# Ten normalising steps on a third engine, and a new written-out order: a one-core transformer block on Trainium2

## The chip, the core and the metric

The kernel runs on one core of a Trainium2 chip. A core has engines that work side by side and wait for one another through semaphores: TensorE (PE, matrix products, with weight loads PEld), VectorE (DVE), ScalarE (ACT), GpSimd (POOL) and SyncE (SP), which issues the transfers. The metric is the device time of one execution in microseconds (us). Every engine executes its own instructions in the order in which the program lists them.

## The reference

One block over x, 2048 positions by 512 channels, in bfloat16, with shift, scale and gate rows computed from a condition vector `c`:

```python
h = _layernorm(x) * (1 + ca) + sa
x = x + ga * _A_ref(h, A_wqkv, A_wo)     # attention over 8 keys: positions s, s-2, ..., s-14
h = _layernorm(x) * (1 + cb) + sb
x = x + gb * _B_ref(h, ...)              # layernorm again, then an MLP over the POSITIONS:
                                         # u = gelu(h^T w1 + b1), y = u w2 + b2
```

The attention has 32 heads of 16 channels. The MLP mixes the 2048 positions through 1792 hidden units, so that it needs all positions of the normalised h.

## The kernel before

The positions come in 16 tiles of 128 rows and in 4 chunks of 4 tiles. Every tile passes three normalisations, so there are 48 normalising steps, each of one 128x512 tile:

- `ln1n0` to `ln1n15`: the first layernorm, from `xx` into `n_sb`. PE then transposes a chunk (`tr`), and the eviction `hT` applies scale and shift.
- `t0` to `t15`: the second layernorm, from the updated `xx` into `h2`. `aff` on DVE then applies scale and shift to the whole chunk in two products.
- `h3_0` to `h3_15`: the MLP's own layernorm, from `h2` into `h3`, which the MLP's matmuls read.

A normalising step needs mean and reciprocal deviation, from `ln1s` and `ln3s` (statistics), `rstd` (ACT) and `nb` (DVE).

For each chunk, PE makes q, k and v (`qkvq`, `qkvk`, `qkvv`), evicted by `evq`, `evk`, `evv`. DVE multiplies q with the 8 shifted keys in four large key products (`qk0_0` to `qk0_3` in chunk 0, one 128x4096 product each). PE sums them within heads (`red`), DVE takes the maximum (`max`), PE subtracts it (`sub`), ACT takes the exponential (`exp`), PE sums (`sum`), `rb` and `smul` divide, `a2_` spreads the weights over partitions, `a2ev` evicts them. Copies of v shifted by position are made by 16 transfers a chunk (`vd`); DVE multiplies them with the weights (`pv`, four a chunk), PE sums (`pvacc`), `oev` evicts, and `wo` projects. `x1ev` adds the result to x. When `x1ev` stands on ACT, the addition of the old x is one more matmul with the identity in `wo`; on DVE it is part of the step.

The MLP's first layer (`mlp1_0_..` over the first 8 tiles, `mlp1_1_..` over the others) runs in between as soon as `h3` tiles are there: `mlp1_0_10_0` reads tiles 0 to 3. `park` keeps its first half; `gadd`, `gelu`, `gbm` finish it, `mlp2` is the second layer, `fin` and `st_out` write the result. PSUM is four slots of two banks (`ps`), which all these steps share.

The order is written out by hand in the string `ORDER`: one word for each step, with the engine after a colon where a step can run on more than one (`v` DVE, `a` ACT, `g` POOL), and the PSUM slot for the steps that open one. `schedule` (line 147) walks it, and the steps are issued in that order, so that it sets the order on each engine and in SP's queue of transfers.

Of the kernel before, what the change touches and what calls it, by code (L numbers as in the profile page):

```python
# [8 lines left out]
ALU = mybir.AluOpType  # L9
# [5 lines left out]
S, D, H, DH, NW, DIL, F = 2048, 512, 32, 16, 8, 2, 1792  # L15
# [14 lines left out]
ln1n0:v modcols_h ln1n1:a nb1_0_2 ln1n3:v modcols1 ln1n2:v ld_wo1 tr0_00:2 tr0_02 ld_wmod5 modcols_cp tr0_10:3 hT0_0:v  # L30
tr0_12 ln1s7:a warm1:1 hT0_2:v hT0_1:v ld_x3 hT0_3:v qkvk0_0:0 ln1s6:a ln1s5:v qkvk0_0b qkvk0_2:2 ld_wmod2 ln1s4:v
evk0_0:a sc_rep rstd1_1_0 ln1s10:v ld_wo2 qkvk0_1:1 evk0_2:a ld_wo3 nb1_1_0 ln1s11:v qkvq0_0:3 ln1n5:a ln1n7:v
qkvq0_2:0 ln1s8:v evk0_1:a ln1n4:a khalo1 ln1s9:v ld_b1 evq0_0:a ln1n6:v rstd1_2_0 ld_wmod4 qk0_0 tr1_10:2 evq0_2:a
ld_wmod3 tr1_00:1 qkvq0_1:3 hT1_2:a ld_wo0 hT1_0:a qkvv0_0:0 nb1_2_0 qk0_2 hT1_3:a evq0_1:a hT1_1:a qkvv0_2:2 evv0_0:a
qk0_1 ln1n10:a qkvq1_0:3 evv0_2:a ln1n8:v ln1s15:a vd0_020 qk0_3 qkvk1_0:1 vd0_001 vd0_011 evq1_0:a red0_0:0 vd0_021
evk1_0:a ln1s12:v red0_1 vd0_000 red0_2 ln1s14:a ln1n11:v vhalo1 red0_3 qk1_0 vd0_131 qkvk1_2:2 vd0_010 ln1n9:a
vd0_121 ln1s13:a vd0_030 qkvq1_2:3 max0 ld_b2 evk1_2:a qk1_1 sub0 evq1_2:a qkvv1_0:1 khalo2 vd0_031 exp0 vd0_101 qk1_2
rstd1_3_0 vd0_111 sum0 tr2_00:2 vd0_130 rb0 red1_0:3 hT2_0:a vd0_120 red1_1 nb1_3_0 smul0 vd0_110 evv1_0:a red1_2
qk1_3 a2_0:0 vd0_100 hT2_1:a tr2_10:1 a2ev0:a qkvv1_2:2 hT2_2:a pv0_0 ln1n14:a red1_3 hT2_3:a modrows:0 ln1n13:a
qkvq2_0:1 pv0_1 mrow_ev evv1_2:a bc0 ln1n12:a biascols:0 vd1_130 pvacc0_0:2 biascols_cp ln1n15:a max1 pvacc0_1 vd1_021  # L40
evq2_0:a vd1_100 tr3_00:0 pv0_3 vd1_010 sub1 oev0_1:a qkvv2_0:1 vd1_011 exp1 vd1_020 vd1_030 pv0_2 hT3_0:a sum1
vd1_000 qkvk2_0:2 evv2_0:a vd1_001 hT3_1:a vd1_031 gmul rb1 vd1_110 pvacc0_2:1 evk2_0:a pvacc0_3 vd1_120 tr3_10:0
smul1 vd1_101 oev0_3:a qk2_1 a2_1:3 vd1_131 hT3_2:a wo2:2 vd1_111 a2ev1:a vd1_121 wo3:1 x1ev2:a bc1 qk2_0 bc2 hT3_3:a
wo0:3 x1ev3:a vhalo2 x1sq2 wo1:2 bc3 pv1_0 x1sq3 qkvq3_0:0 x1ev1:a x1ev0:a x1sq1 pv1_1 pvacc1_0:1 x1sq0 qkvk2_2:2
rstd2_0_0 evq3_0:a nb2_0_0 pv1_2 pvacc1_1 evk2_2:a qkvv2_2:3 t0:a khalo3 ld_w1_0_1 t1:a t2:v pv1_3 qkvq2_2:0 t3:a
oev1_1:a pvacc1_2:2 evv2_2:a aff0_0 pvacc1_3 qkvk3_0:1 evq2_2:a vd2_120 vd2_030 oev1_3:a vhalo3 qk2_2 vd2_020
ln3s0_3:a wo5:3 vd2_010 wo4:0 vd2_021 x1ev5:a vd2_011 evk3_0:a qk2_3 wo7:2 ld_w1_0_3 x1ev4:a vd2_000 wo6:3 x1sq5
vd2_131 x1ev7:a vd2_121 ln3s0_0:v red2_0:1 x1sq4 red2_1 vd2_031 ln3s0_2:v red2_2 vd2_111 x1sq7 red2_3 ln3s0_1:v
# [5 lines left out]
red3_3 mlp1_0_11_4 mlp1_0_10_4 max3 vd3_120 mlp1_0_31_4 park0_1:a mlp1_0_01_4 pv2_1 sub3 pvacc2_0:1 exp3 mlp1_0_00_4
pv2_2 vd3_101 sum3 vd3_100 pvacc2_1 rb3 vd3_121 mlp1_0_30_4 oev2_1:a vd3_130 smul3 mlp1_0_60_0:3 park0_3:a vd3_110
pv2_3 a2_3:1 ld_w1_0_4 pvacc2_2:2 vd3_111 a2ev3:a mlp1_0_61_0 vd3_131 pv3_0 ld_w1_1_5 pvacc2_3 mlp1_0_60_4 oev2_3:a
ld_w1_0_5 mlp1_0_61_4 park0_0:a pv3_1 wo9:1 park0_6:a wo10:2 wo11:0 x1ev9:v ld_w1_1_3 x1ev10:v wo8:3 x1sq9 x1ev11:v
x1sq10 pvacc3_0:1 ld_w1_1_0 x1ev8:v pvacc3_1 x1sq11 mlp1_0_20_0:2 pv3_2 x1sq8 ld_w1_1_1 mlp1_0_40_0:0 rstd2_2_0
oev3_1:a mlp1_0_21_0 ld_w2_2 nb2_2_0 t11:v mlp1_0_40_4 t8:a pv3_3 t10:a mlp1_0_21_4 t9:a mlp1_0_20_4 aff2_0 pvacc3_2:3
ld_w1_1_2 park0_2:a pvacc3_3 mlp1_0_41_0 oev3_3:a mlp1_0_41_4 ld_w2_0 ln3s2_1:v ln3s2_0:a wo12:1 ln3s2_2:v wo13:2  # L60
park0_4:a ln3s2_3:v wo14:3 x1ev13:v rstd3_2_0 wo15:0 x1ev12:v x1sq13 mlp1_0_50_0:2 x1ev14:v x1sq12 ld_w2_7 nb3_2_0
x1ev15:v mlp1_0_51_0 rstd2_3_0 h3_10:v x1sq14 mlp1_0_50_4 nb2_3_0 h3_11:v ld_w1_1_4 h3_8:v t13:a h3_9:v mlp1_0_51_4
t12:v x1sq15 aff3_0 mlp1_1_50_0:1 rstd2_3_2 ld_w1_1_6 park0_5:a mlp1_1_51_0 nb2_3_2 t14:v ln3s3_1:a mlp1_1_30_0:3
t15:v aff3_2 ld_w2_1 mlp1_1_10_0:0 ln3s3_0:a mlp1_1_31_0 ln3s3_3:v mlp1_1_11_0 ln3s3_2:v rstd3_3_0 mlp1_1_00_0:2
ld_w2_3 nb3_3_0 rstd3_3_2 h3_12:v h3_13:a nb3_3_2 mlp1_1_01_0 h3_14:v h3_15:v xb1 mlp1_1_00_4 mlp1_1_10_4 ld_w2_5
mlp1_1_01_4 mlp1_1_50_4 gadd0 mlp1_1_11_4 gelu0 mlp1_1_30_4 gadd1 gelu1 mlp1_1_20_0:2 gelu3 mlp1_1_20_4 gelu2 gbm3
mlp1_1_31_4 gbm1 mlp1_1_40_0:0 gadd3 mlp1_1_21_0 gbm0 gelu6 mlp1_1_21_4 gelu7 gbm6 mlp1_1_51_4 gadd2 mlp1_1_41_0 gadd5
gelu5 mlp1_1_41_4 gelu4 gbm5 mlp1_1_40_4 gelu11 gbm2 gbm7 mlp1_1_60_0:3 gelu10 gadd4 mlp1_1_60_4 gbm11 gelu9
mlp1_1_61_0 gbm10 gbm4 gelu8 gbm9 mlp1_1_61_4 gbm8 xb3 mlp2_3_0_0:2 gadd6 gelu13 gelu12 mlp2_0_0_0:1 gbm12 xb0 gbm13
xb2 mlp2_0_12_0 mlp2_2_0_0:0 mlp2_2_12_0 mlp2_3_12_0 mlp2_5_0_0:3 fin3_0 fin0_0 st_out0_0 ld_w2_4 mlp2_7_0_0:2 xb4  # L70
fin2_0 st_out2_0 mlp2_1_0_0:1 st_out3_0 ld_w2_6 xb7 mlp2_1_12_0 mlp2_7_12_0 fin1_0 mlp2_6_0_0:0 xb6 st_out1_0 fin7_0
st_out7_0 mlp2_6_12_0 mlp2_11_0_0:1 fin6_0 xb11 st_out6_0 xb5 mlp2_10_0_0:2 mlp2_11_12_0 mlp2_4_0_0:0 fin11_0 xb10
st_out11_0 mlp2_4_12_0 xb15 mlp2_10_12_0 mlp2_8_0_0:1 fin10_0 fin4_0 st_out4_0 mlp2_13_0_0:2 mlp2_13_12_0 mlp2_5_12_0
# [157 lines left out]
def kernel(  # L231
# [16 lines left out]
    nc = _OrderedNC(tc, 1)  # L248
# [297 lines left out]
    def build_chunk(ch):  # L546
# [232 lines left out]
        for (g0, g1) in groups:  # L779
# [81 lines left out]
    for fc in range(NFC):  # L861
# [102 lines left out]
```

## Time and profile before

Three runs took 199.56 to 200.11 us, with a median of 199.91. One execution was taken by the profiler:

| what | value |
|---|---|
| the profiled execution's time | 199.6 us |
| its span, first to last instruction | 197.9 us |
| PE busy | 190.3 us (96%) |
| DVE busy | 156.5 us (79%) |
| ACT busy | 125.7 us (64%) |
| POOL busy | 4.3 us (2%), all before 5.7 us |
| first key product on DVE (`qk0_0`) starts | 16.94 us |
| last normalising step on DVE ends | 128.7 us |

The profile gives busy time for each engine, the same in 40 slices of the span, the chain of work that ended last, and groups of equal instructions with the mean duration of one. Nearly every instruction is put down to line 183, a helper that records operations, so that steps are told apart by tiles and shapes: `prod<-q_sb,k_c` is a key product, `pvb<-a2sb,vD` a value product, `h<-h,mv,rs` an `h3` step. A group's mean duration is longer than what the step takes from its engine, because an instruction begins before the one ahead of it has fully ended.

### The profile page before, as it was taken

How to read it: one execution, taken by the hardware profiler on the slowest of the kernel's cores; microseconds unless marked ns; L12 is line 12 of the kernel's file. 1: busy time of each engine (PE TensorE's matmuls, PEld its weight loads, DVE VectorE, ACT ScalarE, POOL GpSimd, SP SyncE). 2: the span in 40 equal slices, each digit the busy share in tenths (PEclk: the TensorE clock that was granted, in tenths of full speed). 3: DMA queues.
4: the chain of work that ended last, by engine and by line, in shares of the span. 5: the costliest groups of instructions: out<-in, count | busy, mean ns of one | idle time of the engine just before them, and what ended most of it. 6: DMA issues, size and time to landing. Idle time of an engine off the chain costs nothing.

```text
span 197.9 us, 3368 instructions
## 1 busy us (share of the span) xinstructions
PE 190.3 (96%) x1270; PEld 89.4 (45%) x1292; DVE 156.5 (79%) x209; ACT 125.7 (64%) x243; POOL 4.3 (2%) x30
## 2 busy tenths in 40 slices
PE   7999999999999999979999999999999999999994
PEld 2656545444444445424434444444444444444452
DVE  1899999999999999999999999946894515261554
ACT  3799999999999999994777999934732000000000
POOL 7100000000000000000000000000000000000000
DMA  5999965547972589696499999998000069000212
GB/s 189 364 337 325 262 148 123 165 109 177 168 126 50 161 231 230 199 216 139 109 198 271 293 284 296 288 296 227 3 0 0 27 183 297 27 27 27 83 50 82
DMA packets 45331, 33.58 MB, mean 170 GB/s; under 512 B 5252, under 2 KB 42756, under 8 KB 45316
## 3 DMA queue, kind: packets, MB, share of 16 engines
q1 hardware_dynamic: 45036, 32.85, 65.5%
q10 hardware_dynamic: 280, 0.53, 0.7%
q8 instruction: 10, 0.16, 0.4%
q14 instruction: 5, 0.04, 0.1%
HBM read 22.03 MB, written 2.10 MB: 122 GB/s over the span
## 4 chain that ended last, share of the span: by engine, by line
PE 54%; ACT 6%; DVE 4%; DMA 2%; issue 1%
PE ps L183 54%; DVE h L183 2%; DMA vD<-v_c 2%; ACT junk L183 2%; ACT h L183 1%; DVE gT L183 1%; ACT v_c L183 1%; DVE pvb L183 1%; ACT ee L183 1%; ACT a2sb L183 0%; ACT k_c L183 0%; ACT q_sb L183 0%; ACT lv L183 0%; DVE k_c L183 0%; ACT rb L183 0%
## 5 line engine op out<-in xcount | busy, mean ns | idle before, releaser
L183 DVE TENSOR_TENSOR pvb<-a2sb,vD 128x4096 bf16<-128x4096 bf16 x16 | 36.1, 2286 | 0.1
L183 PE MATMUL ps<-h,wst 128*128 128x512 bf16 x123 | 29.0, 379 | 0.6 <-ACT a2sb L183 0.2
L183 DVE TENSOR_TENSOR prod<-q_sb,k_c 128x4096 bf16<-128x4096 bf16 x9 | 20.5, 2287 | 0.3 <-ACT q_sb L183 0.3
L183 PEld LDWEIGHTS <-wst 128*128 128x128 bf16 x128 | 12.0, 98 | 16.6 <-issue 3.2
L183 PE MATMUL ps<-gT,vD 128*128 128x512 bf16 x83 | 19.1, 379 | 0.1
L183 DVE TENSOR_TENSOR q_sb<-ps,q_sb 128x512 bf16<-128x512 f32 x8 | 5.5, 688 | 14.2 <-PE ps L183 13.7
L183 PE MATMUL ps<-woq,o_sb 128*128 128x512 bf16 x61 | 15.3, 379 | 0.2
L183 PE MATMUL ps<-hTb,w_q 128*128 128x512 bf16 x63 | 15.1, 379 | 0.1
L183 PE MATMUL ps<-hTb,w_v 128*128 128x512 bf16 x60 | 14.8, 380 | 0.3
L183 PE MATMUL ps<-hTb,w_k 128*128 128x512 bf16 x62 | 14.9, 380 | 0.1
L183 PEld LDWEIGHTS <-w_q 128*128 128x128 bf16 x96 | 10.2, 108 | 10.6 <-issue 0.8
L183 PEld LDWEIGHTS <-o_sb 128*128 128x128 bf16 x106 | 10.2, 98 | 9.9 <-ACT o_sb L183 0.3
L183 DVE TENSOR_TENSOR k_c<-ps,k_c 128x512 bf16<-128x512 f32 (+1 forms) x9 | 5.6, 629 | 11.0 <-PE ps L183 11.0
L183 PEld LDWEIGHTS <-vD 128*128 128x128 bf16 x116 | 9.3, 97 | 10.4
L183 PEld LDWEIGHTS <-w_v 128*128 128x128 bf16 x80 | 8.5, 111 | 9.5 <-issue 2.3
L183 PE MATMUL ps<-gT,pvb 128*128 128x512 bf16 x53 | 12.6, 379 | 0.2
L183 ACT ACTIVATE junk<-xx,su 128x512 bf16<-128x512 bf16 x16 | 11.6, 722 | 1.6 <-DVE xx L183 1.3
L183 PEld LDWEIGHTS <-w_k 128*128 128x128 bf16 x80 | 8.5, 111 | 8.9 <-issue 1.3
L183 PE MATMUL ps<-gT,prod 128*128 128x512 bf16 x55 | 12.4, 379 | 0.1
L183 ACT ACTIVATE gT<-n_sb,b1col 128x512 bf16<-128x512 f32 x8 | 5.3, 714 | 7.7 <-DVE n_sb L183 7.7
L183 PEld LDWEIGHTS <-ident 128*128 128x128 bf16 (+1 forms) x75 | 6.4, 103 | 7.6 <-issue 2.4
L183 DVE BATCH_NORM_STATS2 st<-xx 128x6 f32<-128x512 bf16 x10 | 6.8, 680 | 3.8 <-DMA xx<-in_A_x_dram 3.8
(109 smaller groups left out, 318.5 us busy)
## 6 DMA issues: line engine op xcount, KB each, us to landing
vD<-v_c SPq DMA_DIRECT2D x64, 131.5 KB, 4.6
wst<-in_B_w_dram SPq DMA_DIRECT2D x8, 512.0 KB, 5.7
vD<-in_B_w_dram SPq DMA_DIRECT2D x3, 896.0 KB, 8.3
wst<-in_w_mod_dram SPq DMA_DIRECT2D x4, 512.0 KB, 10.1
prod<-in_B_w_dram SPq DMA_DIRECT2D x2, 896.0 KB, 8.9
pvb<-in_B_w_dram SPq DMA_DIRECT2D x2, 896.0 KB, 10.1
xx<-in_A_x_dram SPq DMA_DIRECT2D x3, 512.0 KB, 8.5
w_q<-in_B_w_dram SPq DMA_DIRECT2D x2, 512.0 KB, 5.0
```

The costliest lines, as they stand in the source:

```text
L183: r = fn(*a, **k)
```

## The change

The normalising step gets a third form, on POOL, with the same instruction as on DVE (`tensor_scalar` with two per-partition scalars). Ten steps use it: `ln1n4`, `ln1n5`, `ln1n10`, `ln1n13`, `t5`, `t7` (ACT before) and `h3_1`, `h3_2`, `h3_8`, `h3_9` (DVE before). `ORDER` is new from the first transposes on. In it, besides the moves to POOL:

- from DVE to ACT: the statistics `ln1s8`, `ln1s12`, `ln3s1_0`, `ln3s1_1`, the norms `t2`, `t11`, `h3_0`, `h3_3`, `h3_4`, `h3_10`, and `x1ev10`
- from ACT to DVE: the statistics `ln1s15`, `ln3s1_2`, `ln3s1_3` and the norms `ln1n9`, `t0`, `t4`, `t10`, `t13`, `h3_5`
- on every engine and in SP's queue steps stand in another order. Behind the first key product: `qk0_1` ahead of `qk0_2`, `modrows` ahead of `sum0`, `biascols` behind the second chunk's projection; in SP's queue the blocks of `w_mod` ahead of `ld_x3`, and `ld_w1_0_2`, `ld_w1_0_4` behind the last `vd3` copies.

POOL's order is `ln1n5 ln1n4 ln1n10 ln1n13 t5 t7 h3_1 h3_2 h3_9 h3_8`, behind the constants that it makes at the start. The diff of the step, and of one stretch of the order in which four of the ten stand:

```diff
@@ -378,15 +379,15 @@
         add("dve", 0.14, f, reads=reads, writes=writes, name=name, lat=0.08)
 
     def norm(dst, src, rs_ap, nb_ap, reads, nbkey, writes, name, mean_ap=None):
-        if mean_ap is None:
-            def f_dve():
-                nc.vector.tensor_scalar(dst, src, rs_ap, nb_ap, op0=ALU.mult, op1=ALU.add)
-        else:
-            def f_dve():
-                nc.vector.tensor_scalar(dst, src, mean_ap, rs_ap, op0=ALU.subtract, op1=ALU.mult)
-        alts = [("dve", _ts4(D, 2), f_dve),
+        def f_ts(eng):
+            if mean_ap is None:
+                eng.tensor_scalar(dst, src, rs_ap, nb_ap, op0=ALU.mult, op1=ALU.add)
+            else:
+                eng.tensor_scalar(dst, src, mean_ap, rs_ap, op0=ALU.subtract, op1=ALU.mult)
+        alts = [("dve", _ts4(D, 2), lambda: f_ts(nc.vector)),
                 ("act", _act(D, 2, False), lambda: nc.scalar.activation(dst, src, ACT.Identity, scale=rs_ap,
-                                                                        bias=nb_ap))]
+                                                                        bias=nb_ap)),
+                ("pool", 0.75, lambda: f_ts(nc.gpsimd))]
         return G.add_any(alts, reads=list(reads) + [nbkey], writes=writes, name=name, lat=0.1)
...
-nb2_1_0 qkvv3_2:3 h3_2:v h3_3:v t7:a h3_1:v h3_0:v t6:a qk3_0 qkvk3_2:0 t5:a ld_w1_0_6 t4:a evv3_2:a sum2 aff1_0 rb2
...
+qk3_1 x1sq6 x1sq4 red2_2 rstd2_1_0 red2_3 evv3_0:a nb2_1_0 qkvv3_2:3 ln3s0_0:v t5:g t6:a max2 t7:g rstd3_0_0 ld_w1_0_6
+t4:v evv3_2:a sub2 nb3_0_0 aff1_0 vd2_001 qkvk3_2:1 exp2 vd2_030 vd3_001 h3_0:a sum2 vd2_110 h3_3:a qkvq3_2:2 h3_1:g
+ln3s1_2:v vd3_020 evk3_2:a h3_2:g vd3_030 ln3s1_3:v rb2 vd2_131 qk3_0 mlp1_0_10_0:3 evq3_2:a vd3_031 mlp1_0_30_0:1
```

More of the change, by code (lines that the diff above doesn't have):

```diff
@@ L29 @@
 warm0:3 ld_w0 silu_exp ln1s1:a silu_dve halo0 ln1s2:v ln1s3:v rstd1_0_0 modcols0:0 ld_w2 nb1_0_0 rstd1_0_2 warm3:1
[L30 to L48, printed above, removed]
@@ L54 @@
[L54 to L73, printed above, removed]
@@ new lines @@
+evk0_0:a qkvk0_2:1 ln1s11:v ld_wo2 rstd1_1_0 ld_wo3 sc_rep ln1s8:a ld_x3 nb1_1_0 ln1s9:v ln1n5:g qkvq0_0:3 ln1s10:v
+ln1n4:g evk0_1:a ld_wmod2 qkvq0_1:0 ln1n7:v evq0_0:a ln1n6:v rstd1_2_0 qkvq0_2:2 qk0_0 evq0_1:a evk0_2:a tr1_00:3
+evq0_2:a tr1_10:0 khalo1 qk0_1 qkvv0_2:1 ld_wo0 hT1_2:a hT1_0:a hT1_3:a qkvv0_0:2 nb1_2_0 qk0_2 hT1_1:a evv0_2:a
+qkvq1_0:0 evv0_0:a ln1n11:v ln1n10:g ln1s15:v ln1s13:a vd0_111 qkvk1_0:3 ln1n9:v vd0_121 qk0_3 vd0_110 evq1_0:a
+vd0_001 red0_0:1 evk1_0:a vd0_010 red0_1 ln1n8:v red0_2 ln1s14:a vd0_021 qk1_0 red0_3 vd0_020 qkvq1_2:2 vd0_000
@@ new lines @@
+vd3_011 ln3s1_1:a vd3_010 mlp1_0_31_0 smul2 ln3s1_0:a mlp1_0_11_0 qk3_2 red3_0:0 a2_2:2 rstd3_1_0 red3_1 a2ev2:a
+nb3_1_0 qk3_3 red3_2 h3_6:a mlp1_0_00_0:2 h3_7:a mlp1_0_01_0 h3_4:a h3_5:v red3_3 pv2_0 mlp1_0_11_4 mlp1_0_10_4 max3
+mlp1_0_00_4 vd3_120 park0_1:a vd3_021 mlp1_0_01_4 pv2_1 vd3_100 sub3 pvacc2_0:3 exp3 mlp1_0_30_4 pv2_2 park0_0:a
+vd3_131 sum3 vd3_110 pvacc2_1 rb3 vd3_121 mlp1_0_60_0:2 oev2_1:a vd3_000 smul3 mlp1_0_61_0 vd3_101 pv2_3 mlp1_0_61_4
+ld_w1_0_2 vd3_130 a2_3:0 vd3_111 pvacc2_2:3 a2ev3:a ld_w1_0_4 pvacc2_3 mlp1_0_60_4 oev2_3:a pv3_1 ld_w2_4 mlp1_0_31_4
@@ new lines @@
+x1ev14:v ld_w1_1_6 mlp1_0_50_4 h3_10:a x1ev15:v h3_8:g rstd2_3_0 mlp1_0_51_0 x1sq14 nb2_3_0 bc3 t12:v mlp1_0_51_4
+t13:v x1sq15 ld_w1_1_4 aff3_0 mlp1_1_00_0:3 rstd2_3_2 park0_5:a mlp1_1_01_0 ld_w2_5 nb2_3_2 t15:v ln3s3_0:a t14:v
+mlp1_1_50_0:1 aff3_2 mlp1_1_30_0:2 ln3s3_1:a mlp1_1_31_0 ln3s3_3:v mlp1_1_51_0 ln3s3_2:v ld_w2_3 rstd3_3_0
+mlp1_1_10_0:0 nb3_3_0 rstd3_3_2 h3_12:v h3_13:a nb3_3_2 h3_15:v mlp1_1_11_0 h3_14:v mlp1_1_00_4 ld_w2_0 mlp1_1_01_4
+mlp1_1_11_4 gadd0 mlp1_1_10_4 mlp1_1_51_4 gadd1 ld_w2_7 mlp1_1_30_4 gelu2 mlp1_1_50_4 gelu3 mlp1_1_31_4 gelu1 gbm3
@@ L77 @@
+st_out15_0
 """
```

36 lines of the change are left out of this document (29 added, 7 removed).

## The prediction

> **What bounds the kernel now.** I read the page first, then the busy times by stretches, the chain that ended last, the waits of PE, VectorE's line in order of time, and last the groups by form, for prices.
>
> ```profile
> PE 190.3 (96%) x1270; PEld 89.4 (45%) x1292; DVE 156.5 (79%) x209; ACT 125.7 (64%) x243; POOL 4.3 (2%) x30
> PE   7999999999999999979999999999999999999994
> DVE  1899999999999999999999999946894515261554
> ACT  3799999999999999994777999934732000000000
> ```
>
> PE is busy nearly all the time, but until about 88 us VectorE and ScalarE are as full. POOL works only at the start. The shares don't say who leads, so the stretches and the chain come next.
>
> ```profile
> 70.00:80.00 10.00, 9.95 (x70) 4.80 (x70) 9.90 (x15) 9.90 (x25) 0.00 (x0) 1.00 0.92 217
> 80.00:90.00 10.00, 8.42 (x92) 3.61 (x96) 9.90 (x13) 9.84 (x21) 0.00 (x0) 1.00 0.92 215
> 90.00:100.00 10.00, 9.84 (x103) 4.04 (x97) 10.00 (x6) 5.40 (x8) 0.00 (x0) 1.00 0.56 120
> ```
>
> The columns after the stretch are its length, then busy time (and instructions) of PE, weight load, DVE, ACT, POOL. From 80 to 90 us PE falls to 8.42 while DVE and ACT stay full: there the vector work leads and PE waits. The chain agrees: it runs through DVE and ACT from 62 us to 88, and from there on it is PE without a break.
>
> ```profile
> 87.03 0.92 ACT a2sb L183
> 87.95 0.04 issue
> 87.99 0.38 PE ps L183
> ...
> 195.02 0.42 DVE k_c L183
> ```
>
> PE's waits are few, and two of the longest stand in that stretch:
>
> ```profile
> 87.16 0.61 PE L183 MATMUL ps<-gT,group 128*32 128x512 bf16 x8 [0.90 <-DVE gT L183]
> 87.99 1.89 PE L183 MATMUL ps<-h,wst 128*128 128x512 bf16 x7 [0.22 <-ACT a2sb L183]
> ```
>
> The first is red3_1 waiting for qk3_2, the second an MLP block waiting for the eviction a2ev2. So after 88 us about 107 us of PE work follow in one piece. The end moves by what the change does to the moment when the last key products (qk3_2, qk3_3) let PE run through, and by what PE itself gains or loses. PE's gaps before that, read off its line, add to some 3.5 us (without the warm-up): no gain can be larger.
>
> **The change, part by part.** Prices:
>
> ```profile
> L183 DVE TENSOR_TENSOR pvb<-a2sb,vD 128x4096 bf16<-128x4096 bf16 x16 | 36.1, 2286 | 0.1
> L183 DVE TENSOR_SCALAR h<-h,mv,rs 128x512 bf16<-128x512 bf16 x12 | 4.3, 409 | 0.0
> L183 ACT ACTIVATE n_sb<-xx,nb,rs 128x512 bf16<-128x512 bf16 x9 | 7.3, 822 | 0.0
> L183 POOL TENSOR_SCALAR_AFFINE_SELECT stack<-stack 128x32 bf16<-128x32 bf16 x4 | 0.8, 212 | 0.3
> L183 POOL TENSOR_SCALAR_AFFINE_SELECT ident<-ident 128x128 bf16<-128x128 bf16 x1 | 0.3, 292 | 0.1
> L183 POOL MEMSET pvb<- 128x1024 bf16 x1 | 1.0, 951 | 0.0
> ```
>
> Instructions overlap at their ends, so what a step takes from its engine is the distance of starts. Four norms in a row on DVE take 1.29 us (76.74 to 78.03), 0.33 each; four on ACT 2.83, 0.71 each; a product 2.20; a statistic 0.80 on DVE and about 1.55 on ACT.
>
> *The price on POOL* is not in the trace. The select rows give (292-212)/96 = 0.83 ns an element, so 0.61 us for 512. The low end is a memset of 512 by the same slope, 0.53; the high end is two passes of a select, 1.22, since the step multiplies and adds. I take 0.61, the row nearest in kind.
>
> *What DVE and ACT shed.* Six of the ten come from ACT (ln1n4, 5, 10, 13, t5, t7), four from DVE (h3_1, 2, 8, 9). The list also trades steps between DVE and ACT. ACT, up to a2ev2: without five ln1n (ln1n9 goes to DVE), ln1s15, t4, t5, t7 and two statistics ln3s1, with ln1s8, ln1s12, h3_0, h3_3 and two other ln3s1: 8 x 0.71 off, 2 x 0.71 and one statistic more, net 6 x 0.71 - 1.55 = 2.7 us less. So ACT stops binding at a2ev2 and DVE decides. DVE, from the first product of the second chunk (qk1_0, 27.27) to the last key product: four h3 off, t4 on, 3 x 0.33 = 1.0 us less. Earlier DVE sheds ln1s8 and ln1s12 for ln1s15 and ln1n9, 0.47 us, and qk0_0 can start some 0.7 earlier because ACT reaches evq0_0 without two norms ahead of it. But qk1_0 needs evk1_0, and adding up ACT's new row gives its end at about 27.15 against 27.14 now: the early gain is waited away, and I count it nothing. That wait is also cover for ln1n10.
>
> *What POOL does to DVE.* No row shows POOL reading a tensor beside a large DVE product. Bounds: nothing, or its whole 0.61 us each time. Below nothing is excluded, for DVE has no wait that POOL could shorten. The only overlap is a small one: the 4-element TENSOR_SCALAR at 4.94 us, under POOL's long memset, took 224 ns where other 4-element steps took 153 to 163. That is nearer to "they get in each other's way", so I take the whole span, but only where POOL meets products. ln1n4, ln1n5 lie beside statistics of the second group; t5, t7 beside ln3s0_0 and max2 (0.80 + 1.13, one PSUM operand); h3_8, h3_9 beside x1ev14 and x1ev15, which read PSUM: nothing. ln1n10 falls between qk0_1 and qk0_2: 0.61, of which the wait for evk1_0 covers 0.36, leaves 0.25. ln1n13 falls among qk1_3 and pv0: 0.61. h3_1 and h3_2 meet t4, aff1_0 and ln3s1: one and a half of them, 0.9. Together 1.76 (if nothing: 0; at 1.22 apiece about 3.5).
>
> The Trainium skill (SBUF — State Buffer, "SBUF: two separate sides") says that GpSimd and VectorE share one pair of ports, held as an exclusive lock for a whole instruction, also against a VectorE instruction with two SBUF inputs. By that rule the sum is the one below, without it the first rival's; no run here shows it yet.
>
> *New waits.* aff1_0 on DVE now waits for POOL's t5 and t7, and behind it stand ln3s1, qk3_0 and all after. Its cover is ln3s0_0, max2, t4 and nb3 (0.80 + 1.13 + 0.33 + 0.08 = 2.34 us) against 2 x 0.61 and about 0.3 of hand-over: nothing; at 1.22 a step, 0.4. mlp1_0_10_0 on PE waits for h3_1, h3_2; ahead of it PE has two projection blocks (2 x 1.73) and two small steps after max2: nothing. tr1 and tr3 wait for ln1n4, 5, 13, with over a microsecond of ACT norms and evictions beside them: nothing.
>
> *Loads.* ld_x3 goes behind three 512 KB blocks of w_mod in SP's queue; by the page's rates the 6.5 MB up to it have landed by about 21.5 us, and its first reader starts at about 23: nothing; if late, up to 1 us. modrows (0.95 us of PE) and biascols only change places. ld_w1_0_2 waits behind the third chunk's vD copies, landing near 103 for a block at 106.
>
> *PE.* x1ev10 goes to ACT, and wo10 then takes a fifth matmul: 0.22 us, on the path. In the tail DVE sheds x1ev10, h3_8, 9, 10, gains t13, 0.61 + 2 x 0.33 = 1.3 us, which PE's unbroken row doesn't feel.
>
> **Sum**: +1.76 - 1.0 + 0.22 = +1.0 us. Profiled execution: 199.6 us (span 197.9 and 1.7 around it), 0.3 below the median of 199.91. So 200.6 in its terms, 200.9 as a median.
>
> **The rivals.**
> *POOL's steps go beside DVE or find its free windows* (they are short, and statistics and PSUM steps come every few microseconds). Then -1.0 + 0.22 = -0.8: 199.1, faster. For it: ACT's and DVE's relief is on the chain of 62 to 88 us. More of PE's gaps could close: down to 198.4. It decides against my forecast when POOL costs DVE under 0.8 us in all.
> *POOL's steps are slow*, 1.2 us and more: 3.5 + 0.4 - 1.0 + 0.2 = +3.1, 203.0. For it: two operations with pointers, for which no row stands. Against: the slope of the selects.
> *Nothing arrives*: POOL's cost and DVE's relief cancel: 199.9.
>
> **How the numbers follow.** A measurement here tells 0.3% (0.6 us) from no change. Forecast 0.46 (about 0.36 slower, 0.09 same, 0.01 faster; its own range 199.6 to 202), POOL free 0.38 (0.29 faster, 0.09 same), slow POOL 0.13, cancelled 0.03. That is 0.30 faster, 0.21 same, 0.49 slower. The range goes from the free case's far end, 198.4, to a little past the slow one, 203.3.
>
> **What would show it.** If right: products of DVE that follow or meet a POOL step are longer than 2286 ns or start late, by 0.6 us each at ln1n10, ln1n13, h3_2; PE's unbroken row starts about 0.8 later than 88 us; ACT has idle time before a2ev2. If the products keep 2286 ns and POOL's rows are near 0.6 us or stretched, the first rival holds. POOL rows above 1 us, and DVE waiting for POOL ahead of aff1_0, speak for the third. I'd be wrong in kind if the end is set by a load (x3, w1) or by a PE gap after 88 us.

## The result, and the profile after

The changed kernel takes 202.11 us (median of six runs, 201.76 to 203.17) beside 200.01 for the kernel before in the same session: 1.0116 times as long, 95% interval 1.0095 to 1.0137, that is 1.9 to 2.7 us more. The forecast was 1.0 us more. The profiled execution of after took 202.67 us with a span of 200.9 us.

The page, first the busy times, then the 40 slices of DVE, ACT and POOL:

```profile
PE 191.4 (95%) x1293; PEld 89.0 (44%) x1293; DVE 156.1 (78%) x201; ACT 125.2 (62%) x244; POOL 32.9 (16%) x40
DVE  1689999999999999999989999936797415343543
ACT  3689999998999999995758999934822000000000
POOL 7108920391000003900000008000000000000000
```

POOL went from 4.3 to 32.9 us of work for ten steps, over 2.8 us a step where 0.61 was taken. DVE has eight instructions fewer but only 0.4 us less of busy time. The stretch from 80 to 90 us (length, then busy time and instructions of PE, weight load, DVE, ACT, POOL):

```profile
80.00:90.00 10.00, 9.34 (x97) 4.39 (x95) 9.86 (x12) 9.68 (x20) 5.14 (x2) 1.00 0.70 187
```

DVE is as full there as before, and two steps on POOL take 5.14 us. They are on the chain that ended last (start, duration, what):

```profile
79.97 5.18 POOL h L184 x2
85.19 4.16 PE ps L184 x54
89.37 1.03 ACT a2sb L184
90.45 34.44 PE ps L184 x243
```

As before, the eviction a2ev2 releases an unbroken row of PE; it begins at 90.45 us where it began at 87.99. Part of these 2.5 us lies at the very start: the first eviction of the normalised input (hT0_0 on DVE) began at 10.69 us against 9.11, behind loads that vary from execution to execution (among the profiled executions of all runs it began between 9.11 and 11.17 us). From here on I therefore also give T, the span minus the start of hT0_0. T is 188.78 us before and 190.21 after: 1.43 us more by the two profiled executions, somewhat less than the runs' difference.

PE's waits show what is new:

```profile
PE ps L184 <- POOL n_sb L184: 1.0, 1, 1.0
PE ps L184 <- POOL h L184: 0.7, 1, 0.7
```

The first is a transpose of the fourth chunk (tr3_00) waiting at 46.20 us for ln1n13, the second the MLP block mlp1_0_10_0 waiting at 85.19 us for h3_2. POOL's own line in order of time (start, duration, instruction; x2 joins two):

```profile
15.05 4.16 POOL L184 TENSOR_SCALAR n_sb<-xx,mv,rs 128x512 bf16<-128x512 bf16 x2 [9.34 <-ACT rs L184]
20.44 6.07 POOL L184 TENSOR_SCALAR n_sb<-xx,mv,rs 128x512 bf16<-128x512 bf16 x1 [1.23 <-ACT q_sb L184]
38.59 7.55 POOL L184 TENSOR_SCALAR n_sb<-xx,mv,rs 128x512 bf16<-128x512 bf16 x1 [12.08 <-PE ps L184]
77.73 1.52 POOL L184 TENSOR_SCALAR h<-xx,rs,nb 128x512 bf16<-128x512 bf16 x2 [31.59 <-DVE nb L184]
79.97 5.17 POOL L184 TENSOR_SCALAR h<-h,mv,rs 128x512 bf16<-128x512 bf16 x2 [0.73 <-ACT rs L184]
120.73 4.13 POOL L184 TENSOR_SCALAR h<-h,mv,rs 128x512 bf16<-128x512 bf16 x2 [35.59 <-ACT rs L184]
```

Two things stand in it. t5 and t7, which multiply and add (scalars `rs,nb`), take 0.77 us each; the other eight, which subtract and multiply (`mv,rs`), take 2.07 us at the least. And ln1n10 and ln1n13, started while DVE runs one large product after another, take 6.07 and 7.55 us. Where ln1n13 ends tells more. It ends at 46.14 us; 2.07 us earlier, at 44.07, DVE's row of three products with two inputs in SBUF has just come to its end:

```profile
39.71 4.48 DVE L184 TENSOR_TENSOR pvb<-a2sb,vD 128x4096 bf16<-128x4096 bf16 x2
44.12 1.21 DVE L184 TENSOR_REDUCE nm<-ps 128x128 bf16<-128x1024 f32 x1
```

For ln1n10 the same count from its end gives 24.44 us, and DVE's row of products gives way to a norm at 24.57. These ends look as if POOL did nothing until the row let go, and then took its own time; what POOL does within a step the trace doesn't show. The products themselves, and DVE's short norms of the same moments:

```profile
L184 DVE TENSOR_TENSOR pvb<-a2sb,vD 128x4096 bf16<-128x4096 bf16 x16 | 36.2, 2285 | 1.0 <-ACT a2sb L184 0.9
L184 DVE TENSOR_TENSOR prod<-q_sb,k_c 128x4096 bf16<-128x4096 bf16 x9 | 20.4, 2279 | 0.2 <-ACT k_c L184 0.2
16.63 1.41 DVE L184 TENSOR_SCALAR n_sb<-xx,mv,rs 128x512 bf16<-128x512 bf16 x2
24.57 0.78 DVE L184 TENSOR_SCALAR n_sb<-xx,mv,rs 128x512 bf16<-128x512 bf16 x1
```

The products keep their 2285 and 2279 ns. It is the short norms that grow: 0.78 us at 24.57 us (ln1n11) where such a step took 0.41, and 1.41 for the pair at 16.63, beside POOL's ln1n5 and ln1n4.

### The profile page after: what moved, and what is told of

It reads as the page before. It is cut to its first block, busy times and chain, and to the rows that moved or that the text cites. A ratio compares the mean times of both kernels' runs of the same rounds, so it can differ in the third digit from the quotient of the medians.

```text
span 200.9 us, 3414 instructions
## 1 busy us (share of the span) xinstructions
PE 191.4 (95%) x1293; PEld 89.0 (44%) x1293; DVE 156.1 (78%) x201; ACT 125.2 (62%) x244; POOL 32.9 (16%) x40
## 4 chain that ended last, share of the span: by engine, by line
PE 65%; ACT 17%; DMA 5%; DVE 5%; POOL 3%; SPq 2%; issue 1%; ACTq 0%; DVEq 0%
PE ps L184 65%; ACT junk L184 4%; DMA vD<-in_w_mod_dram 3%; POOL h L184 3%; SPq L184 2%; ACT v_c L184 2%; ACT xx L184 2%; DVE prod L184 2%; DMA vD<-v_c 1%; ACT a2sb L184 1%; ACT k_c L184 1%; ACT o_sb L184 1%; ACT h L184 1%; ACT hTb L184 1%; ACT q_sb L184 1%
## 5 line engine op out<-in xcount | busy, mean ns | idle before, releaser
L184 DVE TENSOR_TENSOR pvb<-a2sb,vD 128x4096 bf16<-128x4096 bf16 x16 | 36.2, 2285 | 1.0 <-ACT a2sb L184 0.9
L184 PE MATMUL ps<-h,wst 128*128 128x512 bf16 x128 | 29.8, 379 | 0.9 <-POOL h L184 0.7
L184 POOL TENSOR_SCALAR n_sb<-xx,mv,rs 128x512 bf16<-128x512 bf16 x4 | 17.8, 4448 | 22.7 <-PE ps L184 12.1
L184 DVE TENSOR_TENSOR prod<-q_sb,k_c 128x4096 bf16<-128x4096 bf16 x9 | 20.4, 2279 | 0.2 <-ACT k_c L184 0.2
L184 POOL TENSOR_SCALAR h<-h,mv,rs 128x512 bf16<-128x512 bf16 x4 | 9.3, 2332 | 36.3 <-ACT rs L184 36.3
```

Source lines behind the costliest of these rows:

```text
L184: r = fn(*a, **k)
```

## The experiments

Theory from this profile: POOL costs 2.07 us for a step that subtracts, it is held up behind products, and what it costs DVE and PE is the loss. Rivals: the order itself loses, or a load does. The figures of all runs, with T from each one's profiled execution. T repeats well where the work is the same: after, after_x3 and after_x3k agree within 0.04 us, and prices (below), which differs from before only by steps that nobody waits for, has 188.77. The profiled executions of pool_alone and copies_short are apart: PE's clock was halved in them for some 3 us (see copies_short).

| kernel | ratio to before, 95% interval | T, us |
|---|---|---|
| before | | 188.78 |
| after | 1.0116, 1.0095 to 1.0137 | 190.21 |
| copies | 1.0107, 1.0070 to 1.0143 | 190.58 |
| order_alone | 1.0143, 1.0111 to 1.0175 | 192.04 |
| pool_alone | 1.0282, 1.0242 to 1.0322 | 194.21 |
| four_back | 1.0076, 1.0050 to 1.0101 | 190.33 |
| left_out | 1.0022, 1.0002 to 1.0041 | 188.79 |
| multadd | 1.0051, 1.0031 to 1.0071 | 189.45 |
| copies_short | 1.0129, 1.0086 to 1.0172 | 191.81 |
| after_x3 | 1.0083, 1.0051 to 1.0114 | 190.22 |
| left_out_x3 | 0.9974, 0.9955 to 0.9992 | 189.14 |
| multadd_x3 | 1.0030, 1.0006 to 1.0054 | 188.80 |
| six_x3 | 1.0035, 1.0014 to 1.0057 | 189.77 |
| after_x3k | 1.0069, 1.0042 to 1.0096 | 190.25 |
| left_out_x3k | 0.9955, 0.9925 to 0.9985 | 187.92 |
| multadd_x3k | 0.9977, 0.9954 to 1.0000 | 188.18 |
| multadd_x3k_v | 1.0002, 0.9975 to 1.0029 | 188.49 |

### copies: POOL's load alone

The kernel before, with its order, and ten extra instructions on POOL that do the ten steps once more into a tile that nobody reads:

```diff
+        if name in COPIES:
+            def f_copy():
+                if mean_ap is None:
+                    nc.gpsimd.tensor_scalar(spare[:], src, rs_ap, nb_ap, op0=ALU.mult, op1=ALU.add)
+                else:
+                    nc.gpsimd.tensor_scalar(spare[:], src, mean_ap, rs_ap, op0=ALU.subtract, op1=ALU.mult)
+            G.add("pool", 0.75, f_copy, reads=list(reads) + [nbkey], writes=["c_" + name], name="c_" + name, lat=0.1)
```

> The kernel before, its order and engines untouched; GpSimd makes a second copy of the ten normalising steps into a tile that nobody reads. Theory A (POOL is held off: VectorE's products keep the port, POOL's step waits until they pause, and the loss of the changed kernel comes from those who wait for POOL): the products stay at 2285 ns, copies that meet products last 2 to 7 us, copies beside statistics about 0.75 us, nobody waits for POOL, and the time is that of before, 199.6 to 200.5. Theory B (my forecast's mechanism: each POOL step takes its own time from VectorE): products beside a copy start or end 0.6 to 0.8 us late, and the time is 1.5 to 2.5 us above before, near 202. Theory C (POOL has no part in it, the new order is slower): the time of before and copies of 0.75 us throughout.

1.0107. Nobody waits for POOL here, and DVE's instructions are those of before in the same order, so what DVE loses is contention. Its line in order of time, the same two instructions (second half of aff1_0; the value product pv2_0), first before, then copies:

```profile
81.48 1.23 DVE L183 TENSOR_TENSOR h<-h,sb_bc 128x2048 bf16<-128x2048 bf16 x1
...
89.67 2.28 DVE L183 TENSOR_TENSOR pvb<-a2sb,vD 128x4096 bf16<-128x4096 bf16 x1
```

```profile
82.19 1.59 DVE L183 TENSOR_TENSOR h<-h,sb_bc 128x2048 bf16<-128x2048 bf16 x1
...
91.00 2.27 DVE L183 TENSOR_TENSOR pvb<-a2sb,vD 128x4096 bf16<-128x4096 bf16 x1
```

DVE starts pv2_0 1.33 us later, with hT0_0 at the same time (9.14 against 9.11). It loses 0.3 to 0.4 us at a time, mostly at short steps; one key product (at 21.46 us) is lengthened too, 2.70 us in place of 2.29. So contention between POOL and DVE is real and on the path; that much of the forecast held. Each of the theories was half right: nearly all products keep their length, as A said, and the time rises, as B said. Not all of the 1.07% is time that DVE loses. Four of the eight runs have a granted clock of 0.991 or 0.992 (more on this under copies_short); the other four have a median of 201.68, 0.65% above before. And of the 1.80 us of T only 0.78 come before the end of the fourth chunk's last red group.

### prices: the two forms by themselves

The kernel before with eight POOL steps at the end, twice subtract-multiply, multiply-add, add-multiply, multiply-subtract:

```diff
+            nc.gpsimd.tensor_scalar(spare[:], s_, m_, r_, op0=ALU.subtract, op1=ALU.mult)
+            nc.gpsimd.tensor_scalar(spare[:], s_, r_, m_, op0=ALU.mult, op1=ALU.add)
+            nc.gpsimd.tensor_scalar(spare[:], s_, m_, r_, op0=ALU.add, op1=ALU.mult)
+            nc.gpsimd.tensor_scalar(spare[:], s_, r_, m_, op0=ALU.mult, op1=ALU.subtract)
```

> The kernel before, and behind its last h3 tile, where VectorE is no longer full, eight POOL steps of the same 128x512 tile that nobody reads: subtract-multiply, multiply-add, add-multiply, multiply-subtract, twice. Theory D: forms that subtract or add first last 2.07 us, forms that multiply first 0.77 us, or the one with subtract first alone is slow; the run says which. Theory E: all alike where VectorE leaves them alone.

POOL's line of this kernel in order of time, the second round:

```profile
137.39 2.08 POOL L183 TENSOR_SCALAR spare<-h,mv,rs 128x512 bf16<-128x512 bf16 x1
139.57 0.77 POOL L183 TENSOR_SCALAR spare<-h,rs,mv 128x512 bf16<-128x512 bf16 x1
140.44 1.01 POOL L183 TENSOR_SCALAR spare<-h,mv,rs 128x512 bf16<-128x512 bf16 x1
141.54 2.13 POOL L183 TENSOR_SCALAR spare<-h,rs,mv 128x512 bf16<-128x512 bf16 x1
```

In this order of operations: 2.08, 0.77, 1.01 (0.77 in the first round) and 2.13 us. A form with a subtraction takes 2.1 us, one without 0.8, wherever the subtraction stands. Why is left open. The Trainium skill (GPSIMD Engine Reference, "3.1 Elementwise — side-by-side cycle accounting") gives 769 ns for 512 elements as the best case; the 0.77 us of the multiply-add agrees with that, and the subtracting forms are nearly three times as long.

### left_out, multadd, four_back: which part of the change loses

left_out has the changed order and none of the ten steps (those rows of the tile are not computed; POOL sets them to a constant at the start); multadd does all ten in the form that multiplies and adds (the bias, -mean times the scale, is then computed for their groups as well); four_back puts the four that meet products back on ScalarE and VectorE.

```diff
# left_out
-                ("pool", 0.75, lambda: f_ts(nc.gpsimd))]
+                ("pool", 0.75, lambda: None)]
# multadd
-                ("pool", 0.75, lambda: f_ts(nc.gpsimd))]
+                ("pool", 0.75, lambda: nc.gpsimd.tensor_scalar(dst, src, rs_ap, nb_ap, op0=ALU.mult, op1=ALU.add))]
# four_back, in ORDER
-ln1n10:g ln1n13:g h3_1:g h3_2:g
+ln1n10:a ln1n13:a h3_1:v h3_2:v
```

> The changed kernel with the ten POOL steps left out altogether (their tiles keep old values), its order otherwise untouched: what the new order and the relief of ScalarE and VectorE are worth when POOL costs nothing. Theory A+B (the order gains, POOL's steps take it back, by holding VectorE up and by being waited for): 0.3 to 1.2 us faster than before, 2.5 to 3.3 faster than the changed kernel. Theory C (the order itself is slower): 1.5 us and more above before.

> The changed kernel with one difference: POOL's eight steps that subtract the mean and then multiply are written as multiply and add, with the negated mean times the deviation from the nb step, as ScalarE has them. In a run with VectorE idle the first form took 2.07 us and the second 0.77. Theory D (the size of the loss comes from the slow form): PE's waits for POOL go, VectorE is held up half as long: 1.0 to 2.0 us faster than the changed kernel, 200.0 to 201.0. Theory E (the form does not matter, POOL is held off by VectorE's products all the same): 201.6 to 202.3, with POOL steps of 4 to 7 us beside products as before.

> The changed kernel with the four steps whose POOL rows were longest among those that PE waits for put back: ln1n10 and ln1n13 on ScalarE, h3_1 and h3_2 on VectorE; ln1n4, ln1n5, t5, t7, h3_8, h3_9 stay on POOL. Theory A: PE's waits for POOL (0.97 us at the transposes, 0.66 us at the MLP block) are gone: 1.2 to 2 us faster than the changed kernel, 200.0 to 201.0. Theory B: 0.25 + 0.61 + 0.9 less, about the same gain, but with products that are shorter by it. Theory C: no gain, 202.

With POOL's steps gone altogether the kernel is still not faster than before (1.0022). So in this order POOL costs 0.94% of the time, and the order, which sheds ten steps from ScalarE and VectorE, gains nothing: this I had not forecast, and neither theory of this run had it. DVE's line shows a wait that after did not have (in brackets: the wait before the instruction, and for what):

```profile
25.02 0.69 DVE L184 BATCH_NORM_STATS2 st<-xx 128x6 f32<-128x512 bf16 x1 [1.37 <-DMA xx<-in_A_x_dram]
```

It is the first statistic on the fourth group of x, and ld_x3 is late. In after, DVE comes to this group later because of POOL, and the wait is not seen. multadd has the same wait (1.24 us at 24.70) and loses 0.5% in place of 1.2%: the form of the instruction alone is worth more than half of the loss. multadd's 201.08 us stand at the edge of what theory D expected. four_back's interval just overlaps after's (1.0050 to 1.0101 against 1.0095 to 1.0137), and its T is that of after (190.33 against 190.21): by T, ScalarE and VectorE lose by the four steps what POOL lost. The gain of 1.2 to 2 us that I expected did not come.

### order_alone and pool_alone: one half of the change each

```diff
# order_alone: the order of after
-ln1n4:g ln1n5:g ln1n10:g ln1n13:g t5:g t7:g h3_1:g h3_2:g h3_8:g h3_9:g
+ln1n4:a ln1n5:a ln1n10:a ln1n13:a t5:a t7:a h3_1:v h3_2:v h3_8:v h3_9:v
# pool_alone: the order of before
-ln1n4:a ln1n5:a ln1n10:a ln1n13:a t5:a t7:a h3_1:v h3_2:v h3_8:v h3_9:v
+ln1n4:g ln1n5:g ln1n10:g ln1n13:g t5:g t7:g h3_1:g h3_2:g h3_8:g h3_9:g
```

> The changed kernel's order, with the ten steps back on the engines that they had (six on ScalarE, four on VectorE). ScalarE then has 4.3 us more than in the changed kernel and VectorE 1.3 us. Theory A: without POOL's waits PE gains about 1.6 us, and ScalarE's row takes part of it back: 200.3 to 201.5, below the changed kernel. Theory C: as slow as the changed kernel or slower, 202 to 203.5.

> The order of before, with the ten steps on GpSimd. Theory A: h3_1 and h3_2 stand beside the last key products and aff1 and are held off for 4 us and more, PE waits for them at the first MLP block and for n_sb at the transposes: 1.5 to 4 us slower than before, 201.5 to 204. Theory B: 1 to 2 us slower, with longer products. Theory C: not slower than before, 199 to 200.

Each half is slower than the whole, and slower than I expected. The new order with the ten steps on their old engines overloads ScalarE: PE waits 2.0 us for exponentials (`ee`) and 0.8 for an eviction of k. The old order with the steps on POOL pays 2.8%; part of that is PE's clock, which all six runs show below 1.0 (0.983 or 0.992; see copies_short). There VectorE does what I had put at "nothing, or 0.4": it stands still for POOL ahead of aff1_0. Rows of POOL, DVE and PE:

```profile
81.33 2.07 POOL L183 TENSOR_SCALAR h<-h,mv,rs 128x512 bf16<-128x512 bf16 x1
83.38 0.77 POOL L183 TENSOR_SCALAR h<-xx,rs,nb 128x512 bf16<-128x512 bf16 x1
84.18 1.23 DVE L183 TENSOR_TENSOR h<-h,ab_bc 128x2048 bf16<-128x2048 bf16 x1 [3.48 <-POOL h L183]
91.11 1.05 PE L183 MATMUL ps<-gT,group 128*32 128x512 bf16 x8 [3.27 <-DVE gT L183]
```

The first two rows stand beside an idle DVE and still take 2.07 and 0.77 us, so this is POOL's own price. The new order avoids that wait, by starting t5 and t7 ahead of h3_1 and h3_2.

### copies_short: the copies in the short form

```diff
-                if mean_ap is None:
-                    nc.gpsimd.tensor_scalar(spare[:], src, rs_ap, nb_ap, op0=ALU.mult, op1=ALU.add)
-                else:
-                    nc.gpsimd.tensor_scalar(spare[:], src, mean_ap, rs_ap, op0=ALU.subtract, op1=ALU.mult)
+                nc.gpsimd.tensor_scalar(spare[:], src, rs_ap, nb_ap, op0=ALU.mult, op1=ALU.add)
```

The bias is then needed for every group, so that DVE has four short `nb` steps more than in before and copies (213 instructions against 209).

> The kernel before with ten extra POOL steps that nobody reads, as in the run called copies, all in the multiply-add form. With the slow form these copies made VectorE's row 1.3 us later by its last key product. Theory D: POOL is busy a third as long, VectorE is late by 0.3 to 0.7 us there, and the time is 0.3 to 0.9 us above before. Theory E: 1.3 us late again, 2 us above before.

1.0129, no better than copies. This run doesn't say that the short form is as dear. In its profiled execution PE waits 2.48 us for qk3_2, and the matmuls behind that wait are slow (PE's line: a block of which seven matmuls are recorded takes 3.21 us, where the row of before at 87.99 has seven in 1.89):

```profile
88.94 0.61 PE L183 MATMUL ps<-gT,group 128*32 128x512 bf16 x8 [2.48 <-DVE gT L183]
89.49 3.21 PE L183 MATMUL ps<-h,wst 128*128 128x512 bf16 x7
```

The granted clock of that execution is 0.992 over the span, and 0.50 in each stretch of 1 us from 90 to 93 us; in pool_alone's it is 0.50 from 91 to 94. So PE ran at half its clock there, and that is why its matmuls were slow. Three of its six runs have 0.992 and took 203.26 to 204.27 us; three have 1.0 and took 201.65 to 202.05. Copies has both kinds too, 203.29 to 203.62 at 0.991 or 0.992 and 201.43 to 202.56 at 0.999 or 1.0. Which kind an execution is seems to hang on how long PE's wait got (2.0 us in the profiled execution of copies, at a clock of 1.0); that is argued from three profiles and not shown. Where the clock stayed at 0.999 or 1.0, copies has a median of 201.68 us (1.3 above before in its session) and copies_short 201.68 (1.8 above), from four and three runs: here the short form is not seen to be cheaper. In copies_short both halves of aff1_0 are lengthened (1.63 and 1.68 us in place of 1.22 and 1.23), in copies one of them. What contention costs DVE seems to go by the meetings of the two engines, not by the length of POOL's steps; that rests on these two profiles and is not shown.

### The load of x moved ahead

What ld_x3 costs is tried with one change in SP's queue, in after, left_out and multadd:

```diff
-hT0_2:v ld_wmod5
+hT0_2:v ld_x3 ld_wmod5
...
-ln1s8:a ld_x3 nb1_1_0
+ln1s8:a nb1_1_0
```

> The changed kernel with ld_x3 alone moved ahead. There POOL's ln1n10 holds DVE up just before x3 is read, so that most of the late load is hidden: the theory expects a gain of 0.2 to 0.5 us against the changed kernel, ratio to the kernel before 1.009 to 1.011 (1.0116 with ld_x3 behind). If the load were what makes the changed kernel slow, ratio 1.005 or less.

> The changed kernel without POOL's ten steps (those ten rows of the tile are not computed) and with ld_x3 moved ahead in SP's queue: what the order and the relief of DVE and ACT are worth with a POOL that costs nothing and a load that is in time. My forecast had -0.8 us for this, ratio 0.996; if the late x3 was the whole of what was missing (1.002 with ld_x3 where the change has it, 1.37 us of waiting), 0.995 to 0.997. If the ratio stays at 1.002, the order has another loss.

> The changed kernel with POOL's steps in the multiply-add form, and ld_x3 moved ahead of the last w_mod block in SP's queue (behind ld_wmod4). If the late x3 is what eats the order's gain: DVE's wait for x3 at 24.7 us (1.24 us with the multiply-add alone) goes, qk1_0 starts about 1 us earlier, ratio to the kernel before 0.998 to 1.001 against 1.005 for the multiply-add alone. Rival, that the wait is only passed on (the first key product of the second chunk then waits for evk1_0, or a block of w_mod comes late for modrows): ratio 1.004 to 1.006 as before, with a new wait of PE or DVE between 24 and 34 us.

Without POOL's steps the order is now faster than before (0.9974 in place of 1.0022); with the multiply-add form it gains 0.2%, less than expected and within the intervals. (The T of left_out_x3 is from one execution, in which the wait told of below was long; its runs agree better with left_out's being slower.) In after the median hardly moves (202.03 us; the ratio is 1.0083, since before took 200.27 in that session), and T is the same, 190.22 and 190.21: POOL had hidden the load. That both others gain less than the 1.24 to 1.37 us of the wait is the rival I had named, a wait passed on. The DVE line of left_out_x3:

```profile
28.40 2.29 DVE L184 TENSOR_TENSOR prod<-q_sb,k_c 128x4096 bf16<-128x4096 bf16 x1 [1.72 <-DMA k_c<-k_c]
```

The first key product of the second chunk waits for khalo1, a copy of 16 KB that stands behind the 512 KB of ld_wmod2 in SP's queue: issued at 17.95 us, it landed near 28.4.

### Both loads moved

```diff
-ln1n4:g evk0_1:a ld_wmod2 qkvq0_1:0
+ln1n4:g evk0_1:a qkvq0_1:0
...
-evq0_2:a tr1_10:0 khalo1 qk0_1
+evq0_2:a tr1_10:0 khalo1 ld_wmod2 qk0_1
```

> The changed kernel without POOL's ten steps (those ten rows of the tile are not computed), with ld_x3 ahead and the w_mod block ld_wmod2 behind the halo copy khalo1 instead of ahead of it. With ld_x3 alone ahead, qk1_0 waited 1.72 us for khalo1 (issued at 17.95, landed near 28.4). If the queue is what eats the order's gain, that wait goes too and qk1_0 starts when ACT has evicted k_c, near 26.7: 0.8 to 1.7 us less than with ld_x3 alone, ratio to the kernel before 0.989 to 0.994. Rival, that the order gains nothing behind it (PE's waits behind the second chunk's key products take it back): 0.996 to 0.998.

> The multiply-add form on POOL, ld_x3 ahead and ld_wmod2 behind khalo1. With ld_x3 alone ahead qk1_0 waited 0.85 us for khalo1. If the queue: 0.4 to 0.9 us less, ratio 0.998 to 1.001. Rival as for the kernel without POOL's steps: 1.002 to 1.004.

> The changed kernel with both loads moved, POOL's steps as they are. There khalo1 had landed near 27.1 and qk1_0 started at 28.0 without waiting for it, since POOL had held VectorE up. Theory: no further gain, ratio 1.007 to 1.010, as with ld_x3 alone (1.0083); 1.005 or less would say that the loads matter beside POOL too.

left_out_x3k is at 0.9955 and its T at 187.92, 0.86 us below before. That is a smaller gain than the theory's 0.989 to 0.994, and the interval overlaps left_out_x3's, so that what moving ld_wmod2 adds is seen in T (1.22 us) and not in the runs. multadd_x3k is at 0.9977, interval 0.9954 to 1.0000: the change's idea, with the multiply-add form and the loads in time, comes out at or just under the kernel before. after_x3k keeps its T, 190.25; its runs are at 1.0069, and the intervals of the three (after, after_x3, after_x3k) overlap. after_x3k and multadd_x3k differ in the form of POOL's steps alone (and the bias that it needs): 1.0069 against 0.9977, and 2.07 us of T. With the loads in time the form is thus nearly the whole of POOL's cost. multadd_x3k is 0.26 us of T above the kernel without POOL's steps. A short step also meets less: in multadd_x3k ln1n4 is over at 15.95 us, and DVE's two norms of that moment, 1.41 us in after, take 0.38 and 0.40. POOL's groups in multadd_x3k, by form:

```profile
L184 POOL TENSOR_SCALAR n_sb<-xx,rs,nb 128x512 bf16<-128x512 bf16 x4 | 10.1, 2535 | 27.4 <-DVE nb L184 14.2 <-PE ps L184 13.2
L184 POOL TENSOR_SCALAR h<-h,rs,nb 128x512 bf16<-128x512 bf16 x4 | 4.9, 1242 | 38.8 <-DVE nb L184 38.8
```

The same eight steps have means of 4448 and 2332 ns in after. The n_sb mean is still over three times the price, since ln1n10 and ln1n13 are still held up: they take 2.75 and 5.86 us.

### six_x3 and multadd_x3k_v: taking steps back again

```diff
# six_x3, against multadd_x3
-ln1n13:g h3_1:g h3_2:g x1ev10:a
+ln1n13:a h3_1:v h3_2:v x1ev10:v
# multadd_x3k_v, against multadd_x3k
-x1ev10:a
+x1ev10:v
```

> As with the multiply-add form and ld_x3 ahead, but ln1n13 back on ACT, h3_1 and h3_2 back on DVE, and x1ev10 back on DVE (PE's fifth matmul of wo10 falls away, 0.22 us). Theory: the three steps that POOL held longest or handed on late beside DVE's products cost more there than on their old engines, so 0.2 to 0.6 us below the same kernel with all ten on POOL, ratio 0.995 to 0.999. Rival, that each step taken off DVE and ACT is worth its place whatever POOL takes: 0.3 to 0.7 us above it, ratio 1.001 to 1.004.

> The multiply-add form with both loads moved and x1ev10 back on VectorE, so that wo10 takes four matmuls instead of five. My sum has 0.22 us for the fifth, on the path: PE's work behind the last red group 104.6 us instead of 104.8, and a ratio 0.001 below the same kernel with x1ev10 on ScalarE. Rival: VectorE's longer row behind 100 us makes PE wait as much as it saves.

Neither gains. six_x3's T is 0.97 us longer than multadd_x3's, 0.65 of it ahead of the end of the last red group: by T, three normalising steps back on ScalarE and VectorE cost more there than POOL's delay of them, once POOL's form is the short one. The runs can't tell the two apart (1.0035 and 1.0030), but they lie where the rival had them and not below, as the theory asked. And x1ev10 on VectorE saves a matmul but not its time: from the end of the last red group to PE's last matmul it is 105.12 us against 104.80 with x1ev10 on ScalarE (before: 104.56). My 0.22 us for the fifth matmul is not confirmed by taking it away.

## Why the prediction was right or wrong

The direction and the range held; the size did not: +1.0 us was forecast, and 2.1 (1.9 to 2.7) measured. The step that failed is the price of a POOL step, 0.61 us with bounds of 0.53 to 1.22, where eight of the ten steps take 2.07; with it failed the picture of how POOL and DVE collide, and the loads costed at nothing. Step by step, with T taken apart (us, from each profiled execution):

| kernel | from hT0_0 to the end of the last red group | from there to PE's last matmul | from there to the end of the span |
|---|---|---|---|
| before | 81.31 | 104.56 | 2.90 |
| after | 82.19 | 104.75 | 3.27 |
| left_out_x3k | 80.43 | 104.58 | 2.91 |
| multadd_x3k | 80.48 | 104.80 | 2.91 |

The last red group is that of the fourth chunk's key products.

*What bounds the kernel.* Held in the main. PE's row behind the last red group takes 104.56 to 105.12 us in every run, so that a kernel's time is set for the most part by when that group ends: 0.88 of the 1.43 us between before and after. The rest, 0.19 in the row and 0.37 behind it, I had not looked for. PE's gaps between 9 and 88 us add to 2.5 us by the trace, where I had read 3.5.

*DVE's relief, -1.0 us, with +0.22 for PE: -0.78.* The mechanism was right, on a condition I had not seen: with POOL's steps gone and both loads in time, T falls by 0.86 us (187.92 against 188.78), and the last red group ends 0.88 earlier, where I had 1.0. The fifth matmul's 0.22 is not seen: PE's row is 104.58 us with it and 104.56 in before.

*Loads costed at nothing.* This step failed in its own terms. I had ld_x3 landed by 21.5 us, from the page's rates; the statistic on it was released at 24.70 and 25.02 us. I also did not list the copy khalo1 behind one more block of w_mod. Together they cost 0.87 us of T where POOL doesn't hide them (188.79 against 187.92). In the changed kernel itself they are hidden, and moving them leaves T as it is (190.25 against 190.21).

*POOL's price, 0.61 us a step, bounds 0.53 to 1.22.* The step that failed first, and the one that makes the loss. Eight of the ten take at least 2.07 us, outside my bounds, and two 0.77. I had priced "multiply and add" and not looked at which two operations each of the steps does. The select rows could not show a subtraction. With the short form in all ten and the loads in time, 1.0069 becomes 0.9977.

*POOL against DVE, +1.76 us.* This sum was met by luck. At the end of the last red group POOL's steps have cost 1.76 us (82.19 against 80.43), but eight of the ten steps were over three times as long as I had priced them. With steps of 0.77 us, near my price, they have cost 0.05 there (80.48 against 80.43). So the price was far too low and the harm for each us of POOL far too high, and at this point the two errors cancel. T of after stands 2.29 us above left_out_x3k, which has neither POOL's steps nor the late loads. Measured from hT0_0 in the same two traces, the delay is 0.47 us at qk0_0, 1.04 at qk0_3, 0.57 at qk1_3, 1.37 at the first key product of the third chunk, 1.91 at the second of the fourth, 1.76 at the end of the last red group, and 2.29 at the end of the span. So ln1n4 and ln1n5, costed at nothing, take 0.47 (DVE's pair of norms takes 1.41 us in place of 0.71); ln1n10 takes 0.57 where I had 0.25, and 0.47 of the delay so far is given back by qk1_3; around ln1n13 it is 0.80 for 0.61; t5, t7, h3_1 and h3_2 take 0.54 in place of 0.9; and 0.5 us more comes behind the last red group, where I had nothing: 0.17 in PE's row and 0.36 behind PE's last matmul (see the last section).

*How they collide.* Here the forecast had the wrong picture. I expected products to be lengthened, or to start late, by a whole POOL step. In after they keep their length, and POOL waits: 7.55 us for ln1n13. DVE loses 0.2 to 0.4 us at a time, at short steps. PE's row did begin 0.88 us later, counted from hT0_0, as the forecast's sign asked (about 0.8); the sign came true without its mechanism. The rule that I had weighed, in the Trainium skill (SBUF — State Buffer, "SBUF: two separate sides"), lets whichever of the two starts first hold the shared ports for its whole instruction. That POOL is held off by a product which started first agrees with this case. That a norm of DVE which meets a running POOL step grows by 0.37 us only (0.78 against 0.41, beside ln1n10), and not by what is left of the step, doesn't follow from it; nor that qk0_0 and the product behind it take 4.48 us from 17.96, as two products do elsewhere (at 39.71), though ln1n4 had started ahead of them and ended at 19.21. Here the measurement decides.

*New waits costed at nothing.* For aff1_0 this held in after. For tr3 and mlp1_0_10_0 it failed: PE waits 0.97 and 0.66 us, because POOL, held up behind products, hands ln1n13 and h3_2 on late. The cover I had named was real, but for a step of 0.61 us and not for one of 7.55.

*The rivals.* "Slow POOL" had the right cause. Its price of 203.0 us is nearer to the measured 202.11 than my 200.9, but it rests on a slip: at 1.22 us apiece my terms add to 3.9 and not 3.5, since the cover of 0.36 us doesn't grow with the step. Redone, it gives 203.4, which is no nearer. "POOL beside or in free windows" was right about the products. The outcome mixes the two: POOL's steps are slow, and most of that length runs beside DVE's work without hurting it.

*What the ledger leaves.* By T: -0.86 for the relief, +2.29 for POOL, nothing more for the loads: +1.43. The twelve runs of after_x3k, which has the same T as after, agree: their median is 1.43 us above before's in that session (201.55 against 200.12). The six runs of after say 1.9 to 2.7 us. The 0.5 us and more by which they exceed T is not accounted for; the loads ahead of hT0_0, which vary by up to 2 us between executions, are one candidate, not tried.

## What to carry to other kernels

Price a GpSimd step in the very form that it will have, both operations and their order, before deciding what to move: here `subtract, mult` costs 2.07 us and the equivalent `mult, add` with a bias made beforehand 0.77, and that alone was over half the loss, and nearly all of it once the loads were in time. A step on GpSimd that must be ready soon had better not stand among back-to-back two-input products of VectorE: here it waited until they let go, and its consumers with it. When an engine is relieved, look at the DMA queue for what becomes late next, small copies behind large blocks above all; a late load can be hidden by the very delay that one wants to remove.

## What the runs showed of the hardware

- On POOL, `tensor_scalar` over 128x512 bf16 with two per-partition scalars, where no row of DVE's two-input products stood beside it: 2.07 to 2.18 us if one of the operations is a subtraction (2.42 for the first of the row of tests), 0.76 to 0.79 (once 1.01) if not.
- A POOL step beside a row of DVE's products was stretched, to 6.07 and 7.55 us in after and to 10.41 in copies; in after it ended about one step's own time (2.07 us) after the row did. In after the products beside it were not stretched at all. In copies, pool_alone and four_back one product of 32 was, to 2.70, 2.56 and 2.57 us from 2.29.
- PE's matmuls were slow for a few microseconds behind waits of 2.48 (copies_short) and 3.27 us (pool_alone), 3.21 us in place of 1.89 for a block in copies_short; the granted clock was 0.50 there for over 3 us, and 0.992 over the span in both. Behind a wait of 1.98 us (copies) it stayed at 1.0. The Trainium skill (TensorE: Matmul & The Clock Gate, "Part 1: The HAM clock gate") has the array fall to half its clock after an idle window of about 3.4 us; here the wait behind which it was slow was shorter than that.
- Ten POOL steps cost 0.4 to 0.5 us at the very end of the program, though the last such step of after ends over 70 us earlier. From PE's last matmul to the end of the execution, time outside the span included, it is 4.61 to 4.63 us in the profiled executions without such steps, 4.99 to 5.12 with ten, 4.94 with six (four_back) and 4.77 with seven (six_x3). It shows in two places. With the forms of after it is in the span: the stretch behind PE's last matmul takes 3.23 to 3.39 us in place of 2.90 (in after 0.43 us pass between POOL's last two closing instructions, in before 0.08). With all ten in the multiply-add form that stretch stays at 2.90 to 2.92, but the time outside the span is 2.15 to 2.28 us, against 1.66 to 1.79 in left_out. So multadd_x3k's median span is 0.7 us below that of before (197.7 against 198.4) and its median time only 0.2 us (199.90 against 200.12). What takes the time is not in the trace.
